# The tap load moved from SyncE's queue to the head of GpSimd's queue

## The chip, the cores and the metric

The kernel runs on one core of a Trainium2 chip. The metric is the device time of one execution in microseconds (us). The core has five engines with a queue of instructions each: TensorE (PE in the profile; its weight loads are PEld), VectorE (DVE), ScalarE (ACT), GpSimd (POOL) and SyncE (SP). Engines wait for each other, and for transfers, through semaphores. Transfers (DMAs) are issued by SyncE, ScalarE or GpSimd and carried out by 16 DMA engines that all of them share.

## The reference

The inputs are `x` of shape (8, 4096, 192), `weight` of shape (8, 7), `w_in` (192, 2048) and `w_out` (2048, 192), all float32. The output has shape (32768, 192).

```
w   = softmax(weight, axis=-1)                    # 8 heads x 7 taps
att[b, s, h*24 + g] = sum_k w[h, k] * x_padded[b, s + k, h*24 + g]    # causal, 6 zeros ahead
h   = att.reshape(32768, 192) @ w_in              # 2048 wide
g   = where(h > 0, h, exp(min(h, 0)) - 1)         # ELU
out = g @ w_out
```

So it is a short convolution along the sequence with seven softmax weights per head, then two matrix products with an ELU between them.

## The kernel before, in words

The 32768 tokens are cut into 32 blocks of 1024. For each block the kernel makes the convolved tokens (`att`), multiplies them with 16 column groups of `w_in` (the matmuls at L749, into PSUM tiles `H`), applies the ELU in three steps (ScalarE takes the exponential into `E` at L543, GpSimd clips it to at most 1 at L471, VectorE combines it with `H` into `gT` at L610), and multiplies `gT` with `w_out` (L783). The order of TensorE's matmuls is written out once, in the list `steps`, and the other engines follow the same list, so that the second product and the convolution of later blocks are fitted between the matmuls of the first product.

The convolution itself is done on TensorE in two ways. The very first block takes a short way, called the head here: its x is loaded in two halves of 512 tokens into `xf` (the function `load_first`, L340; ScalarE's queue takes half 0, SyncE's half 1), cast to bfloat16 into `xh` (ScalarE at L490 half 0, VectorE at L578 half 1), transposed by TensorE (L649 for the few halo columns, L662 for the rest), copied to `xT`, and multiplied with `Dg`, which holds the taps on diagonals (L682). All later blocks use a banded matrix `Tm`, made from the taps through a small DRAM buffer `conv_taps`, and x tiles `xg` (L727).

The taps are needed by both ways. They start as `wh`, an 8 x 7 float32 tile loaded from `weight`. The softmax is run by VectorE and ScalarE in turn: maximum (L562), difference (L564), exponential (ScalarE, L488), reciprocal (L568), product into `zt` (L570). When `zt` is there, TensorE spreads it to all partitions (L643, after nine warm-up matmuls at L638), VectorE builds `Dg`, and SyncE writes it to `conv_taps` (L805), waits for that, and loads `Tm` (L810).

Each engine does its own work in order, which sets the following sequences around the change:

- SyncE: load of `wh`, load of half 1 of the first x, store of zeros to `conv_taps` (waits for VectorE's `zw`), store of the taps (waits for `zt`), load of `Tm`, and then the loop over `steps` with loads of x, transposes of `att` and stores of the output.
- GpSimd: two selects that make the identity matrix `ident` (L431) and the spreading matrix `sel` (L440), a wait until `wh` has landed (`W(s_wd, 16)`), six loads of `w_in` (L425), two of `xg` for block 1 (L398), the load of `w_out`, two of `xg` for block 2, and then the loop of clips, with copies of x to bfloat16 in DRAM in between.
- VectorE: six memsets, `mask` (waits for `ident`), a wait for `s_wd`, the softmax steps, the cast of half 1 of x, `Dg`, and copies.
- ScalarE: load of half 0 of x, a table load, the exponential of the softmax (waits for VectorE), the cast of half 0, and copies.

The semaphore `s_wd` counts the landing of `wh`; GpSimd and VectorE wait for it. The semaphores `s_xl[0]` and `s_xl[1]` count the landings of the two halves of the first x, `s_wp` the end of `zt`.

Of the kernel before, what the change touches and what calls it, by code (L numbers as in the profile page):

```python
# [54 lines left out]
def bass_lightweight_conv__then__act_elu_kernel(  # L55
# [167 lines left out]
    with ExitStack() as stack:  # L223
        def sbuf(name, shape, dt):
            return stack.enter_context(nc.sbuf_tensor(name, shape, dt))
# [4 lines left out]
        def sema(name):  # L230
            return stack.enter_context(nc.semaphore(name))
# [6 lines left out]
        wh = sbuf("wh", [HEADS, KSIZE], FP32)  # L238
# [23 lines left out]
        s_wd = sema("s_wd")  # L262
# [50 lines left out]

        def x_ready(W, s, part):
            if s <= NXB:
                W(s_x[s % NXB][part], 16)
            else:
                W(s_xq[s % NXB][part], 32 * ((s - 1) // NXB))

# [24 lines left out]

        def conv_read(W, m):
            W(s_ce, 2 * (m + 1))

# [16 lines left out]

        def singles_done(W, acc):
            x_ = final[acc]
# [26 lines left out]
        @block.gpsimd  # L393
        def _gpsimd(g: bass.BassGpSimd):
            W = Waits(g)

            def load_x(s, part):
                g.dma_start(  # L398
                    xg[:, s % NXB, WPG * part : WPG * (part + 1), :],
                    bass.AP(  # L400
                        tensor=x_flat.tensor,
                        offset=(s * SUP + GS * part - PAD) * D,
                        ap=[[D, P], [TOK * D, WPG], [1, D]],
                    ),
                ).then_inc(s_x[s % NXB][part], 16)

            def pad_x(s):
                x_ready(W, s, 0)
                g.memset(xg[0:PAD, s % NXB, 0, :], 0.0).then_inc(s_z)

            def copy_x(s):
                W(s_cv, 4 * (s - NXB - 1) + 1)
                if s == NXB + 1:
                    g.dma_start(  # L414
                        xb[s * SUP - 8 : s * SUP, :], x_flat[s * SUP - 8 : s * SUP, :]
                    ).then_inc(s_xb[s % 2], 16)
                g.dma_start(  # L417
                    xb[s * SUP : (s + 1) * SUP, :].rearrange("(p t) d -> p (t d)", p=P),
                    x_flat[s * SUP : (s + 1) * SUP, :].rearrange("(p t) d -> p (t d)", p=P),
                ).then_inc(s_xb[s % 2], 16)  # L420

            def load_w_in(k, halves):
                c0, c1 = WCOLS[k]
                for r in halves:
                    g.dma_start(  # L425
                        w_in[HP * r : HP * (r + 1), :, c0:c1],
                        moe_w_in.rearrange("(p j) f -> p j f", j=3)[:, :, c0:c1],
                    ).then_inc(s_w[k], 16)

            W(s_one, 1)  # L430
            g.affine_select(  # L431
                out=ident[:],
                in_=ident[:],
                pattern=[[-1, P]],
                compare_op=ALU.is_equal,
                fill=0.0,
                base=0,
                channel_multiplier=1,
            ).then_inc(s_id)
            g.affine_select(  # L440
                out=sel[:].rearrange("p (r h c) -> p r h c", r=2, h=HEADS),
                in_=sel[:].rearrange("p (r h c) -> p r h c", r=2, h=HEADS),
                pattern=[[0, 2], [-1, HEADS], [0, 8]],
                compare_op=ALU.is_equal,
                fill=0.0,
                base=0,
                channel_multiplier=1,
            ).then_inc(s_id)
            W(s_wd, 16)
            load_w_in(0, (0, 1))  # L450
            load_w_in(1, (0, 1))
            load_w_in(2, (0, 1))
            load_x(1, 0)
            load_x(1, 1)
            g.dma_start(
                w_out.rearrange("p (q r) d -> p q (r d)", r=RUN),
                moe_w_out.rearrange("(q p r) d -> p q (r d)", p=FC, r=RUN),
            ).then_inc(s_w[3], 16)
            load_x(2, 0)
            load_x(2, 1)  # L460
            for n in range(NP):
                s, i = divmod(n, NQ)
                if i == X_PAD and s + 2 < NS and (s + 2) % SPB == 0:
                    pad_x(s + 2)
                if i == X_COPY and s and s + 3 < NS:
                    copy_x(s + 3)
                if n == X_LATE[0]:
                    copy_x(3)
                for u in range(2):
                    W(s_exp, 2 * n + u + 1)  # L470
                    g.tensor_scalar(  # L471
                        out=E[:, n % NE, u, :],
                        in0=E[:, n % NE, u, :],
                        scalar1=1.0,
                        scalar2=0.0,
                        op0=ALU.min,
                        op1=ALU.max,
                    ).then_inc(s_clp)
# [315 lines left out]
        @block.sync  # L794
        def _sync(sy):
            W = Waits(sy)
            sy.dma_start(wh[:], weight[:, :]).then_inc(s_wd, 16)
            load_first(sy, 1)
            W(s_zw, 1)
            sy.dma_start(  # L800
                bass.AP(tensor=taps.tensor, offset=0, ap=[[(HEADS + 2) * CW, BANDS], [(HEADS + 1) * CW, 2], [1, CW]]),
                zw[0:BANDS, 0 : 2 * CW].rearrange("p (a e) -> p a e", a=2),
            ).then_inc(s_band, 16)
            W(s_wp, 1)
            sy.dma_start(  # L805
                bass.AP(tensor=taps.tensor, offset=CW, ap=[[CW, HEADS], [(HEADS + 2) * CW, BANDS], [1, CW]]),
                zt[:, :].unsqueeze(1).to_broadcast([HEADS, BANDS, CW]),
            ).then_inc(s_band, 16)
            W(s_band, 32)
            sy.dma_start(  # L810
                Tm[:, :, :].rearrange("p h e -> p (h e)"),
                bass.AP(tensor=taps.tensor, offset=CW + TAP + KSIZE - 1, ap=[[(HEADS + 2) * CW - P // BANDS, BANDS], [-1, P // BANDS], [1, HEADS * CW]]),
            ).then_inc(s_band, 16)

            def load_cast(s):
                W(s_cv, 4 * (s - NXB))
                W(s_xb[s % 2], 16 * ((s - 1) // 2 + (s % 2)))
                if s > NXB + 1:
                    W(s_xb[(s - 1) % 2], 16 * ((s - 2) // 2 + ((s - 1) % 2)))
                for part in range(2):  # L820
                    row = s * SUP + GS * part - PAD
                    for w0, w1, rows in ((0, WPG - 1, P), (WPG - 1, WPG, GS - TOK * (WPG - 1) + PAD)):
                        v0 = WPG * part
                        sy.dma_start(
                            xg[0:rows, s % NXB, v0 + w0 : v0 + w1, :],
                            bass.AP(
                                tensor=xb.tensor,
                                offset=(row + TOK * w0) * D,
                                ap=[[D, rows], [TOK * D, w1 - w0], [1, D]],
                            ),  # L830
                        ).then_inc(s_xq[s % NXB][part], 16)

            for x_, op in enumerate(steps):
                if op[0] == "h" and op[2:] == (0, 0):
                    s, i = divmod(op[1], NQ)
                    if i == X_LOAD and s and s + 3 < NS:
                        load_cast(s + 3)
                    if op[1] == X_LATE[1]:
                        load_cast(3)
                elif op[0] == "c" and op[3:] == (1, HB - 1):  # L840
                    m, b = op[1:3]
                    s = m // 2 + 1
                    if m % 2 and b:
                        conv_read(W, m)
                        for u in range(2):
                            W(s_h[u], NQ * (s - 1))
                        turn_att(sy, s)
                elif x_ in stops:
                    acc = acc_of(op)
                    t, half, kb, g = acc  # L850
                    if (t, half) == (last, 1):
                        if (kb, g) != (1, 1):
                            taken(W, acc)
                            out_group(sy, t, half, g, kb)
                    else:
                        taken(W, acc)
                        out_group(sy, t, half, g)
            for b in range(2):
                sy.wait_ge(s_out[b], 32 * NS + 32 * b)
# [28 lines left out]
```

## Time and profile before

| | |
|---|---|
| time, median of 3 runs | 726.29 us (725.12 to 727.17) |
| the profiled execution's own time | 724.59 us |
| its span in the profile | 722.5 us |
| TensorE busy | 714.7 us, 99% of the span |
| ScalarE, VectorE, GpSimd busy | 91%, 90%, 87% |
| granted TensorE clock | 1.0 |
| issue of `wh` (SyncE's queue), start and length | 0.80 us, 0.40 us |
| issue of half 1 of the first x (SyncE's queue) | 1.26 us, 0.36 us |
| issue of half 0 of the first x (ScalarE's queue) | 0.81 us, 0.38 us |
| GpSimd's first load of `w_in` | 2.44 us |

The span is the time between the first and the last recorded instruction; the time of a run is a little longer than that. Starts are counted from the beginning of the span. "SPq" and "ACTq" in a row are the queues of SyncE and ScalarE, where only the issue of a transfer is shown and not the transfer; a row of GpSimd for a DMA likewise shows the issue. A bracket at the end of a row gives how long the engine had been idle and what ended that. In the lists of DMA queues, q0 carries what GpSimd issues.

### The profile page before, as it was taken

The numbers are of one execution on the slowest core, as the hardware profiler recorded it, in microseconds if no ns is written. First come the engines' busy times: TensorE is split into PE (matmuls) and PEld (weight loads), VectorE is DVE, ScalarE is ACT, GpSimd is POOL, SyncE is SP. The second block draws the span as 40 slices with busy tenths as digits, with TensorE's granted clock in tenths as the row PEclk, the third lists the DMA queues.
The fourth block names the chain that finished last, engine by engine and source line by source line (L and its number), as shares of the span: only waits on it lengthen the run. The fifth ranks groups of instructions, "written<-read, shape, count | busy, mean of one in ns | idle before, by whom it ended". The sixth has DMA issues, their size and how long they took to land.

```text
span 722.5 us, 28723 instructions
## 1 busy us (share of the span) xinstructions
PE 714.7 (99%) x11866; PEld 620.3 (86%) x11866; DVE 651.1 (90%) x1043; ACT 655.9 (91%) x1286; POOL 631.0 (87%) x1078
## 2 busy tenths in 40 slices
PE   8899999999999999999999999999999999999997
PEld 4598888888888888888888888888888888888897
DVE  5899999999999999999999999999999999999994
ACT  6899999999999999999999999999999999999994
POOL 8889988889888889888889888898888898888893
PEclk9999999999999999999999999999999999999999
DMA  9854533654534644444645335545346455432212
GB/s 179 129 117 86 112 78 88 117 103 83 103 83 95 116 91 96 94 93 95 116 82 106 83 83 116 105 82 111 75 95 117 93 93 100 88 94 71 58 36 67
DMA packets 130051, 69.16 MB, mean 96 GB/s; under 512 B 94128, under 2 KB 128688, under 8 KB 129456
## 3 DMA queue, kind: packets, MB, share of 16 engines
q1 hardware_dynamic: 123760, 52.08, 30.5%
q0 software_dynamic: 5872, 14.75, 14.9%
q8 instruction: 93, 1.52, 0.9%
q10 hardware_dynamic: 288, 0.49, 0.2%
q14 instruction: 38, 0.31, 0.1%
HBM read 43.51 MB, written 36.61 MB: 111 GB/s over the span
## 4 chain that ended last, share of the span: by engine, by line
PE 95%; DMA 2%; POOL 1%; ACT 1%; issue 0%; DVE 0%; ACTq 0%
PE ops L783 51%; PE H L749 40%; PE H L727 3%; DMA xg<-in_x_dram 2%; PE H L783 1%; POOL w_in L425 1%; POOL E L471 1%; ACT E L543 0%; DVE gT L610 0%; POOL xg L398 0%; ACT csb L521 0%; POOL x_cast L414 0%; POOL x_cast L417 0%; POOL sel L440 0%; ACT osb L513 0%
## 5 line engine op out<-in xcount | busy, mean ns | idle before, releaser
L610 DVE SCALAR_TENSOR_TENSOR gT<-E,H 128x512 f16<-128x512 f32 x1024 | 645.3, 683 | 56.9 <-POOL E L471 49.7
L471 POOL TENSOR_SCALAR E<-E 128x512 f32<-128x512 f32 x1024 | 606.1, 616 | 79.5 <-ACT E L543 75.6
L543 ACT ACTIVATE E<-H 128x512 f32<-128x512 f32 x1024 | 565.2, 612 | 49.5 <-PE H L749 44.9
L749 PE MATMUL H<-att,w_in 64*128 64x512 bf16 x3072 | 602.9, 377 | 1.2 <-DVE gT L610 1.0
L783 PE MATMUL ops<-w_out,gT 64*128 64x192 f16 x8064 | 587.0, 243 | 0.0
L783 PEld LDWEIGHTS ops<-w_out,gT 64*128 64x128 f16 x8064 | 516.5, 94 | 54.5 <-PE ops L783 29.4
L749 PEld LDWEIGHTS H<-att,w_in 64*128 64x128 bf16 x3072 | 258.0, 94 | 20.0 <-DVE gT L610 6.5
L727 PE MATMUL H<-xg,Tm 64*128 64x240 bf16 x480 | 87.6, 263 | 0.3 <-DVE gT L610 0.3
L521 ACT ACTIVATE csb<-H 128x480 bf16<-128x480 f32 x120 | 70.7, 589 | 0.0
L513 ACT ACTIVATE osb<-ops 128x384 f32<-128x384 f32 x125 | 61.0, 488 | 7.3 <-PE ops L783 5.7
L727 PEld LDWEIGHTS H<-xg,Tm 64*128 64x128 bf16 x480 | 38.2, 93 | 16.1 <-issue 0.6
L417 POOL DMA_DIRECT2D x_cast<-in_x_dram x29 | 15.6, 538 | 0.0
L783 PE MATMUL H<-w_out,gT 64*128 64x192 f16 x128 | 6.4, 243 | 0.0
L783 PEld LDWEIGHTS H<-w_out,gT 64*128 64x128 f16 x128 | 5.7, 94 | 0.0
L638 PE MATMUL ops<-zw 128*128 128x512 bf16 x9 | 4.0, 631 | 1.2 <-DVE zw L553 1.2
L602 DVE COPY osb<-ops 128x384 f32<-128x384 f32 x1 | 0.6, 558 | 4.3 <-PE ops L783 4.3
L727 PE MATMUL ops<-xg,Tm 64*128 64x240 bf16 x16 | 3.0, 264 | 1.3 <-ACT csb L521 0.7
L699 PE MATMUL ops<-zw 64*128 64x512 bf16 x12 | 4.2, 376 | 0.0
L425 POOL DMA_DIRECT2D w_in<-in_moe_w_in_dram x6 | 4.0, 664 | 0.2 <-DMA wh<-in_weight_dram 0.2
L638 PEld LDWEIGHTS ops<-zw 128*128 128x128 bf16 x9 | 1.2, 143 | 3.2 <-issue 1.9
L727 PEld LDWEIGHTS ops<-xg,Tm 64*128 64x128 bf16 x16 | 0.9, 94 | 3.2 <-ACT csb L521 1.5
L398 POOL DMA_DIRECT2D xg<-in_x_dram x4 | 3.5, 878 | 0.0
(49 smaller groups left out, 29.8 us busy)
## 6 DMA issues: line engine op xcount, KB each, us to landing
out_dram<-osb SPq DMA_DIRECT2D x126, 192.0 KB, 3.3
x_cast<-in_x_dram POOLq DMA_DIRECT2D x29, 384.0 KB, 5.1
xg<-x_cast SPq DMA_DIRECT2D x58, 192.0 KB
xg<-x_cast SPq DMA_DIRECT2D x58, 26.2 KB
xg<-in_x_dram POOLq DMA_DIRECT2D x4, 240.0 KB, 13.3
w_in<-in_moe_w_in_dram POOLq DMA_DIRECT2D x2, 384.0 KB, 10.4
w_out<-in_moe_w_out_dram POOLq DMA_DIRECT2D x1, 768.0 KB, 14.6
w_in<-in_moe_w_in_dram POOLq DMA_DIRECT2D x2, 288.0 KB, 6.3
```

Source lines behind the costliest of these rows:

```text
L417: g.dma_start(xb[s * SUP : (s + 1) * SUP, :].rearrange("(p t) d -> p (t d)", p=P), x_flat[s * SUP : (s + 1) * SUP, :].rearrange("(p t) d - ...
L425: g.dma_start(w_in[HP * r : HP * (r + 1), :, c0:c1], moe_w_in.rearrange("(p j) f -> p j f", j=3)[:, :, c0:c1],).then_inc(s_w[k], 16)
L471: g.tensor_scalar(out=E[:, n % NE, u, :], in0=E[:, n % NE, u, :], scalar1=1.0, scalar2=0.0, op0=ALU.min, op1=ALU.max,).then_inc(s_clp)
L513: a.activation(*out_pieces(acc), ACT.Copy).then_inc(s_oev)
L521: return a.activation(csb[:, s % 2, :].rearrange("p (j v h i) -> p h j v i", j=3, v=2 * WPG, h=HEADS)[:, h0 : h0 + HB], bank_of(("c", m, b ...
L543: a.activation(E[:, n % NE, u, :], bank_of(op[:3]), ACT.Exp).then_inc(s_exp)
L610: v.scalar_tensor_tensor(out=gT[:, s % NG3, q, u, :], in0=E[:, n % NE, u, :], scalar=1.0, in1=bank_of(op[:3]), op0=ALU.subtract, op1=ALU.m ...
L638: pe.matmul(ops[:, 0, :], zw[:, 0:P], zw[:], start=True, stop=True)
L699: pe.matmul(ops[:, 1 - rt, :], zw[HP * rt : HP * (rt + 1), 0:P], zw[HP * rt : HP * (rt + 1), :], start=True, stop=True, tile_position=(HP ...
L727: ins = pe.matmul(bank_of(op[:3])[:, n1 * hh : n1 * (hh + 1)], Tm[HP * rt : HP * (rt + 1), h, :], xg[HP * rt : HP * (rt + 1), s % NXB, :, ...
L749: ins = pe.matmul(bank_of(op[:3]), w_in[HP * r : HP * (r + 1), j, RUN * FC * (q // RUN) + q % RUN : RUN * FC * (q // RUN + 1) : RUN,], att ...
L783: ins = pe.matmul(to[:, d0 : d0 + D], gT[HP * rt : HP * (rt + 1), t % NG3, q, g, t0 : t0 + P], w_out[HP * rt : HP * (rt + 1), q, :], start ...
```

## The change

The load of `wh` is taken out of SyncE's queue, where it was the first instruction, and put into GpSimd's queue as its first instruction of the kernel body. Its source, its destination and the semaphore it raises stay the same. SyncE now begins with half 1 of the first x load; GpSimd issues one more transfer, ahead of its two selects, and later still waits for that transfer where it did before. Every line number between the two places grows by one.

```diff
@@ -393,6 +393,7 @@
         @block.gpsimd
         def _gpsimd(g: bass.BassGpSimd):
             W = Waits(g)
+            g.dma_start(wh[:], weight[:, :]).then_inc(s_wd, 16)
 
             def load_x(s, part):
                 g.dma_start(
@@ -794,7 +795,6 @@
         @block.sync
         def _sync(sy):
             W = Waits(sy)
-            sy.dma_start(wh[:], weight[:, :]).then_inc(s_wd, 16)
             load_first(sy, 1)
             W(s_zw, 1)
             sy.dma_start(
```

## The prediction

> **What bounds the kernel now.** I read the page first: TensorE is busy 99% of the span, and 95% of the chain that ended last is matmuls. So most of this kernel can't notice a change at its start, except as a shift of everything. Whether the start is on the path at all is told by the chain of waits in order of time, cut to the first 40 us (start, length, what):
>
> ```profile
> 1.83 0.36 POOL sel L440
> 2.20 0.24 issue
> 2.44 0.84 POOL w_in L425
> ...
> 3.27 3.11 POOL w_in L425 x5
> 6.39 0.90 POOL xg L398
> 7.29 11.57 DMA xg<-in_x_dram
> 18.86 0.14 issue
> 19.00 0.26 PE ops L727
> ```
>
> The head of the path is not the first x load. It is GpSimd: its two selects, six `w_in` loads, the two `xg` loads, then the landing of `xg` at 18.86, for which TensorE stands idle 0.53 us in front of the first convolution matmul (L727). From there the chain goes through the exponentials to 31 us and then stays on TensorE to the end. `load_w_in` stands behind GpSimd's wait for the taps (`s_wd`), so the taps' landing is directly ahead of this path.
>
> The timeline of the first 6 us shows both sides of the edit (start, length, engine, line):
>
> ```profile
> 0.80 0.40 SPq L797 DMA_DIRECT2D wh<-in_weight_dram  x1
> ...
> 1.26 0.36 SPq L340 DMA_DIRECT2D xf<-in_x_dram  x1
> ...
> 2.16 0.15 DVE L562 TENSOR_REDUCE whm<-wh 8x1 f32<-8x7 f32 x1
> ...
> 2.86 0.19 ACT L488 ACTIVATE whe<-wh 8x7 f32<-8x7 f32 x1
> ...
> 3.36 0.22 DVE L570 TENSOR_SCALAR zt<-whe,whr 8x7 bf16<-8x7 f32 x1
> ...
> 3.92 0.84 ACT L490 ACTIVATE xh<-xf 128x768 bf16<-128x768 f32 x1 [0.78 <-DMA xf<-in_x_dram]
> ...
> 5.08 0.56 DVE L578 CAST xh<-xf 128x768 bf16<-128x768 f32 x1 [1.50 <-DMA xf<-in_x_dram]
> ...
> 5.21 0.18 PE L643 MATMUL H<-zt,sel 8*128 8x7 bf16 x1
> ```
>
> The taps, sent at 0.80, have landed by 2.16, when VectorE's reduction runs: at most 1.36 us. SyncE's half of x is cast at 5.08, yet TensorE only leaves its nine warm-up matmuls at 5.2 and still has the tap broadcast (L643) and twelve small halo matmuls ahead of the transposes that read that half.
>
> Last, the table by stretches (stretch, length, busy time of PE, PEld, DVE, ACT, POOL, granted clock, DMA share, GB/s), and then, from the list of DMA queues between 4.0 and 4.4 us, the packets of GpSimd's queue, their MB and their share:
>
> ```profile
> 1.50:2.00 0.50, 0.50 (x2) 0.15 (x1) 0.27 (x3) 0.50 (x1) 0.46 (x2) 1.00 0.52 80
> 2.00:2.50 0.50, 0.50 (x2) 0.15 (x1) 0.47 (x3) 0.50 (x1) 0.26 (x2) 1.00 0.65 166
> ...
> 3.50:4.00 0.50, 0.50 (x3) 0.16 (x2) 0.08 (x1) 0.07 (x1) 0.50 (x2) 1.00 1.03 418
> ...
> 17.00:18.00 1.00, 0.79 (x7) 0.21 (x5) 1.00 (x3) 0.80 (x2) 1.00 (x3) 1.00 1.52 196
> ```
>
> ```profile
> q0 software_dynamic: 22, 0.01, 27.7%
> ```
>
> The DMA engines are idle before 1.5 us, half used to 2.5 and full from then to 24. So `xg` lands when the work queued before it is done; only idle time of the DMA engines in the first microseconds can move it.
>
> **What the Trainium skill says.** "DMA: Bandwidth & Descriptors", section Specifications, puts the first byte at about 1 us on GpSimd's path and 0.6 on SyncE's. Its section "Anatomy of one DMA — SWDGE (gpsimd) path" gives a GpSimd DMA a fixed 2.0 us, mostly the receipt. The trace agrees in kind: a 3 KB copy of GpSimd (`x_cast`, L414) landed 2.8 us after its issue, while the taps by SyncE took 1.36 or less. "Issuing engines are not separate DMA queues" on the same page says that all queues end on the same 16 engines, as the full table shows. "SBUF — State Buffer", section "SBUF: two separate sides", warns that a VectorE operation in a two-port mode keeps GpSimd from writing descriptors. Here VectorE's 0.56 us cast at 5.08 ran beside GpSimd's `w_in` issues and none of those is over 0.84, so I price that at 0 to 0.5 us, inside the bounds below.
>
> **The change part by part.**
>
> *Removed from SyncE: one issue.* Its x load moves from 1.26 to about 0.80, 0.46 us. The engines had (0.48 + 0.35) x 0.5 = 0.41 us free between 1.5 and 2.5; I let x fill all of it. SyncE's x then lands near 4.6. ScalarE's half loses its head start and may land up to 0.5 later, at 4.4.
>
> *Added to GpSimd: one issue of 0.59 (L414) to 0.84 us (the first `w_in` issue, 0.21 longer than the median 0.63).* It starts near 0.8, so the select of `ident`, at 1.54 now, moves to at most 1.7. GpSimd also has an instruction without a row, which the build names a library reload; it stands just before that select, now after the new DMA. In the kernel before it fits between 0.8 and 1.54, so it costs 0 to 0.7. Even then `ident` and `sel` are done by 3.1; VectorE's mask waits for `ident` and TensorE (5.2) for both. They are hidden under the wait for the taps.
>
> *The taps land later.* Latency: lower end 1.36 + 0.4 (the skill's difference in first byte) = 1.8; upper end 3.2, that of the first 96 KB `w_in` load. I take 2.8, from L414: though that one writes to DRAM, the taps now travel while x has the engines full. Landing 3.6 (2.6 to 4.0).
>
> *Behind the taps on VectorE and ScalarE.* From the reduction at 2.16 to the end of `zt` at 3.58 takes 1.42, so `zt` is ready at 5.0 where TensorE wants it at 5.2: hidden by the warm-up, 0.4 late at the upper end. ScalarE's exponential moves to 4.3, and its cast of x behind it from 3.92 to 4.6, ending 5.45; the halo matmuls start 0.15 late. VectorE's cast goes from 5.08 to 5.0. The head thus gains nothing from the earlier x load, and may lose 0.15 (0.6 at the upper end). The first layer-one matmul at 9.9 may shift by that; it is covered by the 0.53 us that TensorE waits for `xg` anyway. SyncE's tap stores and `Tm` load, behind the same `zt`, move 1.4 later; `Tm`'s packets now end before 15, four microseconds before use.
>
> *Behind the taps on GpSimd: six w_in loads, two xg loads, w_out, two xg loads, then its clips.* The first issue moves from 2.44 to 3.6 + 0.24 = 3.84, or +1.4. It is no longer the first on its queue, which gives back 0.21. So GpSimd's packets start 1.2 later, at about 5.25 instead of 4.05. The x traffic left at 4.05 was some 0.26 us of work (65.7% of the 0.4 us stretch, on SyncE's queue); with 0.41 done earlier it ends at 3.9. The engines then idle 5.25 - 3.9 = 1.35, less the 0.41 saved: `xg` lands 0.9 later. Ends: -0.1 at a latency of 1.8, +1.3 at 3.2. `w_in`'s second part, wanted after 12 us, lands about 11 now, a cover of 1 us; `xg` for the next block lands about 25, wanted 26.9, and both move together.
>
> *To the end.* TensorE waits for `xg` with every later matmul behind it, and from 19 to 31 us the chain has no stall long enough to take up 0.9. All of it passes: span 722.5 + 0.9 = 723.4; the profiled execution took 724.59, 2.1 around its span, so 725.5. The median shown, 726.29, stands 1.7 above that execution, so the forecast is 727.2.
>
> **Rivals.** (a) *Hidden after all*: the taps by GpSimd land near 2.6, GpSimd's start hardly moves, and the DMA queue decides. For it: the transfer is 224 bytes. Against it: L414. Time 726.3. (b) *The edit does what its words say*: x half a microsecond earlier and `xg` earlier with it. TensorE could use at most the 0.53 it waits for `xg`: 725.8. Against it: GpSimd's loads would have to start no later than now. (c) *Slower*: the library reload can't begin while GpSimd's own DMA is open. It then starts at 3.6, takes up to 0.7, the selects 0.65, the issue 0.24: `w_in` at 5.2, 2.75 later. GpSimd's packets start at 6.6, idle 6.6 - 3.9 - 0.41 = 2.3, time 728.6. It decides for slower when the first `w_in` issue comes after 5.1; no row shows the reload, so I can't exclude it.
>
> **How the numbers follow.** A measurement of this kernel tells about 0.3%, 2.2 us. Chances: main case 0.6, (a) 0.15, (b) 0.05, (c) 0.15, and 0.05 for something later in the taps' landing than I bound. Only (c), the last and a little of the main case's upper end pass +2.2: slower 0.19; faster 0.03; same 0.78. The range reaches from (b), less run-to-run scatter (725.1 to 727.2 before), to (c): 725.3 to 729.0.
>
> **What would show it.** Right: the reduction on VectorE at about 3.6, GpSimd's first `w_in` at 3.8, TensorE leaving the warm-up at 5.2 still, `xg` landing near 19.8, a longer TensorE wait there, and nothing else changed from 31 us on but the shift. Wrong: the reduction before 2.8, or `ident`'s select after 3, or `xg` landing unchanged while `w_in` starts late, or a shift at 20 us that is gone at 31.

## The result and the profile after

The changed kernel takes 730.08 us in the median of four runs (729.92 to 730.36), the kernel before 726.48 us in four (725.12 to 727.17): a ratio of 1.0052, 95% interval 1.0035 to 1.0070. It is slower by 3.6 us, where 0.9 had been forecast. Of the two profiled executions the one after has a span of 728.1 us, the one before 722.5; that one (724.59 us by its own time) was at the quick end of its kernel, so the difference of the spans, 5.6 us, is larger than that of the medians.

Nearly the whole loss, 5.3 of these 5.6 us, is made in the first 37 us. The chain of waits of the changed kernel, its first 40 us (start, length, what):

```profile
1.34 4.15 DMA wh<-in_weight_dram
...
5.79 3.97 POOL w_in L426 x6
9.76 0.89 POOL xg L399
10.65 13.54 DMA xg<-in_x_dram
...
24.33 0.26 PE ops L728
```

The path goes the same way as before, through GpSimd's loads to the landing of `xg`, but with the taps now at its head: 4.15 us from their issue to their landing at 5.49, where they had landed by 2.16. `w_in` starts 3.35 us later (5.79 for 2.44) and `xg` lands 5.33 later (24.19 for 18.86). The point of the chain where VectorE hands over to TensorE for good is at 36.4 us instead of 31.1. From 40 to 700 us TensorE is busy without a gap in both kernels.

The timeline of the first 7 us, the main rows that answer to those shown of the kernel before:

```profile
0.80 0.39 SPq L340 DMA_DIRECT2D xf<-in_x_dram  x1
...
1.34 0.68 POOL L396 DMA_DIRECT2D wh<-in_weight_dram  x1 [0.83 <-POOLq L873]
...
5.51 0.15 DVE L563 TENSOR_REDUCE whm<-wh 8x1 f32<-8x7 f32 x1 [2.77 <-DMA wh<-in_weight_dram]
...
6.83 0.16 PE L644 MATMUL H<-zt,sel 8*128 8x7 bf16 x1 [1.85 <-DVE zt L571]
```

GpSimd starts its issue at 1.34, half a microsecond after the other two queues; no row shows why. VectorE then waits 2.77 us for the taps, and everything behind it is late: both casts of x (ScalarE's at 6.16 for 3.92, VectorE's at 6.61 for 5.08), and TensorE's tap broadcast at 6.83 instead of 5.21, in front of which TensorE is idle for 1.85 us.

The DMA engines, by the list of DMA issues of the first 3.4 us (KB, us from issue to landing):

```profile
xf<-in_x_dram SPq DMA_DIRECT2D x1, 384.0 KB, 4.2
xf<-in_x_dram ACTq DMA_DIRECT2D x1, 384.0 KB, 4.3
wh<-in_weight_dram POOLq DMA_DIRECT2D x1, 0.2 KB, 4.2
```

and by the same list of the kernel before:

```profile
xf<-in_x_dram ACTq DMA_DIRECT2D x1, 384.0 KB, 3.1
xf<-in_x_dram SPq DMA_DIRECT2D x1, 384.0 KB, 3.8
```

Both halves of x now land at about 5.0 to 5.1 us. Before, they landed at 3.9 and 5.1. So SyncE's half, sent 0.46 us earlier, is there no more than 0.1 us earlier, and ScalarE's half is 1.2 us later. The taps, 224 bytes, land after both.

The table by stretches (columns as in the prediction) shows what that does to the engines that carry the rest. First a row of the kernel before, then rows of the changed one:

```profile
5.00:5.50 0.50, 0.50 (x5) 0.28 (x5) 0.42 (x1) 0.00 (x0) 0.50 (x2) 1.00 0.99 120
```

```profile
5.00:5.50 0.50, 0.00 (x0) 0.00 (x0) 0.00 (x0) 0.00 (x0) 0.00 (x0) 1.00 0.00 0
...
6.00:7.00 1.00, 0.16 (x1) 0.09 (x1) 0.69 (x3) 0.98 (x3) 1.00 (x2) 1.00 0.00 0
...
8.00:9.00 1.00, 0.99 (x19) 0.74 (x15) 0.62 (x1) 0.79 (x2) 1.00 (x2) 0.50 1.05 140
```

The DMA engines, full from 2.5 to 24 us in the kernel before, are empty from 5 to 7 us: x is done, and `w_in`, whose issue only starts at 5.79, shows its first packets at 7.2. TensorE's granted clock (the third figure from the right) falls to half from 8 us, after its idle stretch.

### The profile page after: what moved, and what is told of

The parts are those of the page before. It is cut to its first block, busy times and chain, and to the rows that moved or that the text cites. A ratio compares the mean times of both kernels' runs of the same rounds, so it can differ in the third digit from the quotient of the medians.

```text
span 728.1 us, 28723 instructions
## 1 busy us (share of the span) xinstructions
PE 716.0 (98%) x11866; PEld 621.2 (85%) x11866; DVE 651.6 (89%) x1043; ACT 655.9 (90%) x1286; POOL 631.8 (87%) x1079
## 4 chain that ended last, share of the span: by engine, by line
PE 95%; DMA 2%; POOL 1%; ACT 1%; issue 0%; DVE 0%; ACTq 0%; POOLq 0%
PE ops L784 51%; PE H L750 40%; PE H L728 3%; DMA xg<-in_x_dram 2%; PE H L784 1%; DMA wh<-in_weight_dram 1%; POOL w_in L426 1%; ACT E L544 1%; POOL E L472 0%; POOL xg L399 0%; ACT csb L522 0%; DVE gT L611 0%; POOL x_cast L418 0%; POOL x_cast L415 0%; ACT osb L514 0%
## 5 line engine op out<-in xcount | busy, mean ns | idle before, releaser
L784 PEld LDWEIGHTS ops<-w_out,gT 64*128 64x128 f16 x8064 | 516.5, 94 | 54.5 <-PE ops L784 29.4
L750 PEld LDWEIGHTS H<-att,w_in 64*128 64x128 bf16 x3072 | 258.4, 94 | 21.3 <-DVE gT L611 3.6
```

The source lines that it names most:

```text
L750: ins = pe.matmul(bank_of(op[:3]), w_in[HP * r : HP * (r + 1), j, RUN * FC * (q // RUN) + q % RUN : RUN * FC * (q // RUN + 1) : RUN,], att ...
L784: ins = pe.matmul(to[:, d0 : d0 + D], gT[HP * rt : HP * (rt + 1), t % NG3, q, g, t0 : t0 + P], w_out[HP * rt : HP * (rt + 1), q, :], start ...
```

## The experiments

Two theories of the late taps. A: they share the DMA engines with x, and land with x when they are not ahead of it. B: a first transfer by GpSimd's queue is slow by itself. And two theories of how the delay reaches the end. G: through GpSimd's wait in front of its loads. H: through the late softmax at the head.

### The taps alone on the DMA engines

```diff
 # changed kernel; SyncE, and ScalarE after its table load:
+W(s_wd, 16)
 load_first(...)
```

> The changed kernel, but both halves of the first x are sent only once the taps have landed. If the taps land late because they share the DMA engines with x (theory A), they now land about 2.0 to 2.6 us after GpSimd's issue at 1.34, at 3.4 to 3.9. If a first transfer by GpSimd is slow by itself (theory B), they land where they do in the changed kernel, at about 5.5. The total is no test here, since x comes some 3 us late: 729 to 732 under A.

728.63 us in its one run, beside 725.88 for the kernel before. The chain of waits of this kernel:

```profile
1.33 1.76 DMA wh<-in_weight_dram
3.11 4.43 DMA xf<-in_x_dram
```

By the same queue, from the same start, the taps land at 3.09: 1.76 us after the issue instead of 4.15. So GpSimd's path isn't what is slow; of the 4.15 us, 2.4 go with x being ahead. Its landing is even quicker than theory A had asked. The edit holds back SyncE's store of zeros as well, to 3.55; that this small store isn't the cause is shown by the next run, where it is sent behind the taps and they are late all the same. The second line tells the price of this cure: x itself, landing at 7.54, is now the head of the path. Still, with x 2.4 us later than in the changed kernel, the one run of this kernel is no slower than it.

### The exchange on SyncE's queue, without GpSimd

```diff
 # kernel before, SyncE
-sy.dma_start(wh[:], weight[:, :]).then_inc(s_wd, 16)
 load_first(sy, 1)
+sy.dma_start(wh[:], weight[:, :]).then_inc(s_wd, 16)
```

> The kernel before with two instructions of SyncE's queue exchanged: its half of x first, then the taps; GpSimd issues nothing more. If taps sent beside or behind x land late whatever the queue (theory A), they land near 5, w_in starts near 5.3 and the time is about 729.5 to 730. If GpSimd's path is what is slow (theory B), they land 1.3 us after an issue at 1.25, near 2.6, and the time is 726.5 to 727.

730.58 us (730.34 to 731.12), 1.0063 of the kernel before, interval 1.0048 to 1.0078. The chain of waits, and then VectorE's reduction in the timeline:

```profile
1.24 4.08 DMA wh<-in_weight_dram
```

```profile
5.35 0.15 DVE L562 TENSOR_REDUCE whm<-wh 8x1 f32<-8x7 f32 x1 [3.19 <-DMA wh<-in_weight_dram]
```

The taps take 4.08 us on SyncE's queue too when x goes first, and the whole loss is there, 4.7 us against the kernel before (725.88), with GpSimd's queue untouched. With the first experiment this settles A against B from both sides.

### The taps first on ScalarE's queue

```diff
 # kernel before: taken from SyncE's queue; ScalarE begins with
+a.dma_start(wh[:], weight[:, :]).then_inc(s_wd, 16)
 load_first(a, 0)
```

> The kernel before with the taps at the head of ScalarE's queue instead of SyncE's: SyncE begins with its half of x at 0.80, the taps are first in the other queue, ScalarE's half follows at 1.26. If what counts is that the taps are in a queue ahead of x's packets (theory A), they land near 2.1 and the time is that of the kernel before within 0.7 us. If x sent at the same moment by another queue is enough to hold them back, they land near 5 and the time is about 730.

726.09 us (725.43 to 727.64), 1.0004 of the kernel before, interval 0.9996 to 1.0013: no difference. The chain of waits:

```profile
1.41 3.92 DMA xf<-in_x_dram
...
5.36 0.85 ACT xh L491
...
6.26 0.64 PE H L650 x9
```

VectorE's reduction runs at 2.16, as before, though SyncE's x is sent at 0.80, at the same moment as the taps. So x may be sent beside the taps, not ahead of them. It also bears on what the change wanted: SyncE's half of x goes first here with the taps on time, and nothing is won. But ScalarE's half, from which the halo matmuls are made, goes 0.6 us later for it (1.41 for 0.81), lands at 5.34 and is the head of the path. What SyncE's half would be worth with ScalarE's left where it was isn't tested.

### GpSimd's wait alone

```diff
 # kernel before, GpSimd, with a tile wg and a semaphore s_wg of its own
+g.dma_start(wg[:], weight[:, :]).then_inc(s_wg, 16)
 ...
-W(s_wd, 16)
+W(s_wg, 16)
 load_w_in(0, (0, 1))
```

> The kernel before, with a second copy of the taps loaded at the head of GpSimd's queue into a tile of its own; GpSimd waits for that copy before its w_in loads, and the softmax uses SyncE's copy as before. If GpSimd's late loads carry the loss (theory G), xg lands 3 to 5 us later and the time is about 730, as in the changed kernel, though the softmax is on time. If the late head carries it (theory H alone), the time stays at 726.5.

729.16 us (728.77 to 729.59), 1.0044, interval 1.0028 to 1.0061. Theory G carries 3.3 us with the softmax as good as on time (the tap broadcast is at 5.20). But it isn't `xg` that ends the chain here:

```profile
1.33 3.87 DMA wg<-in_weight_dram
...
7.44 8.70 DMA w_in<-in_moe_w_in_dram
...
16.19 0.39 PE H L752
...
20.65 0.65 PE H L752 x3
```

TensorE, at its first layer-one matmul at 10.49 (10.02 in the kernel before), then waits 3.8 us for the second part of `w_in`. The matmuls after this wait are on the chain too, and from 18 to 20 us their granted clock is 0.50. So a part of the 3.3 us may be the clock's; no run separates the two. The copy of the taps by GpSimd lands at 5.2 here with both x loads where they were in the kernel before: again with x, which was sent ahead of it.

### The head alone: no wait on GpSimd

```diff
 # changed kernel, GpSimd
-W(s_wd, 16)
 load_w_in(0, (0, 1))
```

> The changed kernel without GpSimd's wait for the taps before its loads of w_in; VectorE still waits for them. If the loss goes through GpSimd's loads alone (theory G), w_in starts near 3.0, xg lands near 19.5 and the time is that of the kernel before, 726.5 to 727. If the late softmax at the head carries part of it too (theory H), TensorE reaches its first layer-one matmul near 12.7 instead of 10.0, the convolution about 2.1 us later than before, and the time is about 728.5.

727.81 us (727.41 to 728.46), 1.0025, interval 1.0016 to 1.0035. With GpSimd's loads nearly on time 1.9 us are left, between what G and H had said. The chain shows a third way that neither had:

```profile
1.34 4.37 DMA wh<-in_weight_dram
...
6.93 8.27 DMA conv_taps<-zt
15.22 6.53 DMA Tm<-conv_taps
```

`zt` is late, so SyncE's store of the taps is sent at 6.9, now behind GpSimd's `w_in` packets, takes 8.27 us for 32 KB, and the `Tm` load behind it lands at 21.75, when `xg` has been there for three microseconds. TensorE's wait for it is short, though:

```profile
21.79 0.27 PE L727 MATMUL ops<-xg,Tm 64*128 64x240 bf16 x1 [0.50 <-DMA Tm<-conv_taps]
```

TensorE comes to this place at 21.3 us, where it came at 18.5 in the kernel before. So the late softmax costs about 2 us by itself. `Tm` ends the chain, but by this trace it adds only 0.5 us to the late head, theory H. The head is late by the softmax, and from 9 to 11 us it runs at a clock of 0.50.

### The first cut of TensorE's clock

```diff
-WARM = (9, 1)
+WARM = (13, 1)      # changed kernel
```

> The changed kernel with 13 warm-up matmuls on TensorE in place of 9, so that TensorE is busy until the late taps come, at about 6.7, and its clock is not cut to half from 8 to 11.4 us. If the head is off the path (xg ends it), TensorE reaches its first layer-one matmul about 1 us earlier, near 11.6, and the time stays that of the changed kernel, within 0.5 us of 730. If the cut clock is part of the loss, the time falls by 1 us or more, to 729 or less.

729.92 us (729.80 to 730.17), 1.0056, interval 1.0041 to 1.0071, against 730.08 of the changed kernel. The row of the table by stretches:

```profile
8.00:9.00 1.00, 0.67 (x20) 0.55 (x17) 0.69 (x1) 0.92 (x3) 1.00 (x2) 1.00 1.18 148
```

The clock is whole there now, the first layer-one matmul is at 11.47 instead of 12.66, and the time doesn't move: this cut of the clock and the late head are off the path in the changed kernel. A second cut comes after the wait for `w_in` and stands in both kernels (0.50 from 19 to 21 us). In the changed kernel it is over before TensorE waits 0.83 us for `xg`, so the chain doesn't go through it; the second run of the next experiment doesn't have it.

### xg ahead of the last part of w_in

```diff
 # GpSimd
 load_w_in(1, (0, 1))
-load_w_in(2, (0, 1))
 load_x(1, 0)
 load_x(1, 1)
+load_w_in(2, (0, 1))
```

On the kernel before:

> The kernel before with GpSimd's two xg loads for block 1 ahead of the last part of w_in. In the kernel before TensorE waits 0.53 us for xg; here xg should land near 14 and the last part of w_in near 18.9, wanted near 19.3. A gain of 0.3 to 0.6 us if nothing else binds; none, if the last part of w_in takes xg's place.

724.85 us (723.70 to 726.62), 0.9983, interval 0.9977 to 0.9990: 0.9 us won, a little more than expected, and below both kernels. `xg` is off the path, and in its place stands the very thing the change was after, SyncE's half of x:

```profile
1.25 4.22 DMA xf<-in_x_dram
...
5.49 0.94 DVE xh L578
...
6.48 0.45 PE H L662 x8
```

On the changed kernel:

> The changed kernel with GpSimd's two xg loads for block 1 ahead of the last part of w_in, the same exchange that was worth 0.9 us on the kernel before. If xg alone carries the late start of GpSimd's loads to the end, most of the loss is gone and the time is near 727. If the second part of w_in, for which TensorE waits 2.2 us at 17.1 in the changed kernel, carries it as well, only the 0.8 us that TensorE waits for xg after that is won, and the time is near 729.2: 4.4 above the kernel before with the same exchange.

729.66 us (728.90 to 730.81), 1.0049, interval 1.0036 to 1.0061. That is 0.4 us under the changed kernel's 730.08, and the loss against the kernel before (726.09 here) is still 3.6. In the changed kernel TensorE waits for the second part of `w_in` and then for `xg`:

```profile
17.14 0.39 PE L750 MATMUL H<-att,w_in 64*128 64x512 bf16 x1 [2.22 <-DMA w_in<-in_moe_w_in_dram]
...
24.33 0.26 PE L728 MATMUL ops<-xg,Tm 64*128 64x240 bf16 x1 [0.83 <-DMA xg<-in_x_dram]
```

With `xg` ahead, the chain of waits goes through the second part of `w_in`:

```profile
7.99 9.55 DMA w_in<-in_moe_w_in_dram
17.59 0.39 PE H L750
...
19.77 4.88 DVE gT L611 x8
```

The granted clock is 1.00 from 17 to 24 us, so the loss is there without the second cut of the clock. This part of `w_in` lands at 17.54 us here. By the increments of its semaphore it landed at 17.09 in the changed kernel and at 11.77 in the kernel before. So the late start of GpSimd's loads reaches the end by two ways, and taking one away leaves the other.

### The wait itself, on the kernel before

```diff
 # kernel before, GpSimd
-W(s_wd, 16)
 load_w_in(0, (0, 1))
```

> The kernel before without GpSimd's wait for the taps. The taps land at 2.14 there, before GpSimd has done its two selects at 2.20, so the wait should cost nothing: w_in starts near 2.4 and the time is that of the kernel before within 0.7 us.

725.79 us (724.97 to 726.46), 1.0000, interval 0.9991 to 1.0009. While the taps are first, the wait costs nothing; it only makes GpSimd's loads hostage to their landing.

## Why the prediction was wrong

The forecast was 727.2 with a range to 729.0; measured are 730.1.

**The taps land later: the step that failed.** "Landing 3.6 (2.6 to 4.0)" came from a latency of 2.8, bounded above by 3.2. Measured: 4.15, from an issue at 1.34 and not at 0.80, landing 5.49. Of the 1.9 us between 3.6 and 5.49 the latency makes 1.35 and the later issue 0.54. The step saw that the taps "travel while x has the engines full" and then took its numbers from rows in which that holds less. The 2.8 was a copy at 28.6 us, during which the DMA engines were nearly idle from 29.4 to 30.3. The 3.2 was the first `w_in` load, issued at 2.44, only 2.6 us ahead of x's landing; it landed at 5.6, itself just behind x. In every kernel here in which the taps were sent behind x, the end of x is what bounded them. In the profile before that number could be read: x landed at 5.06. Issue at 1.34, landing with x at about 5.1 to 5.5, would have given `w_in` at 5.3 to 5.8, and by the prediction's own rival (c), which "decides for slower when the first `w_in` issue comes after 5.1", a slower kernel.

**Removed from SyncE: an assumed gain.** "I let x fill all of it", 0.41 us of free DMA time. Nothing came of it: SyncE's half landed at most 0.1 us earlier, and ScalarE's half 1.2 later against the allowed 0.5. The last packet of x begins at 4.58 us, in the kernel before at 4.50; the sum had x done at 3.9.

**Behind the taps on VectorE and ScalarE.** The 1.42 us from reduction to `zt` was near in size (5.51 to 6.68 after, 1.17), but its cover, the warm-up to 5.2, was gone: TensorE stood idle 1.85 us, and from 8 us its clock was cut. That this head is covered by the wait for `xg` held in the changed kernel (the experiment with more warm-up). It doesn't hold once `xg` is on time: without GpSimd's wait the late softmax costs 1.9 us. There `Tm`, "four microseconds before use" in the prediction, had no cover left, with the tap store queued behind `w_in`.

**Behind the taps on GpSimd.** The path was right: `w_in`, then `xg`, then everything. With the right landing the sum of the prediction gives: packets of GpSimd from about 7.2, x done at 3.9, idle 3.3, less 0.41: 2.9, and a time of 729.2; between the medians 3.6 were measured. The 0.41 is the gain that didn't come. `xg` itself was 5.33 later in the profiled executions, more than the idle time of the DMA engines explains (last section). The cover of 1 us claimed for the second part of `w_in` was used up too, and TensorE waited 2.2 us for it.

**To the end.** "All of it passes" was right: 5.33 us at `xg` became 5.34 where TensorE takes over the chain, and 5.6 of span.

**The rivals.** (a) and (b) are refuted: GpSimd's loads started 3.35 us later and the time rose. (c) named the right place with the wrong cause: `ident`'s select runs at 2.12, right after GpSimd's issue and three microseconds before the taps land, so no instruction of GpSimd was held by its open DMA. The time fell to the case given 0.05, "something later in the taps' landing than I bound".

## What to carry to other kernels

A small transfer that many engines wait for belonged ahead of the large ones in time here, on SyncE's queue or on ScalarE's: sent 0.5 us after 768 KB of x had been issued, 224 bytes landed with the end of x, by GpSimd's queue and by SyncE's alike. When a transfer's latency has to be bounded, take the row that was issued into the same traffic, and if there is none, take the end of that traffic. A wait that costs nothing today (GpSimd's, 0.0 us) still ties the loads behind it to what it waits for, so price it by what happens when that comes late.

## What the runs showed that was not expected

The taps landed after x even on a queue of their own. In the list of DMA queues GpSimd's packets, issued by 2.02, first appear between 4.0 and 4.5 us, as x runs out (q1 and q10 carry SyncE's and ScalarE's transfers):

```profile
q10 hardware_dynamic: 41, 0.11, 55.0%
q1 hardware_dynamic: 46, 0.06, 34.3%
q0 software_dynamic: 10, 0.00, 1.1%
```

The Trainium skill ("DMA: Bandwidth & Descriptors", section "Queues, rings and completion order") says that each engine takes the queues in turn by packet, and that the write that raises the semaphore lands only after every earlier write of that engine, across its queues. The second fits every kernel in which the taps were sent behind x: by the semaphores in the trace they landed at 5.3 to 5.7 us (their copy at 5.2), each 0.2 to 0.4 after x. It doesn't explain the delay, which is already in the packets. Whether the first explains it these traces can't tell, for they show neither single DMA engines nor how many rows a turn takes. GpSimd's next load fares alike: the first `w_in`, issued at 2.44 in the kernel before, shows its first packet at 4.1, and with the taps alone, issued at 3.38 behind x, at 6.7. Why they come so late was not tested.

The landing of `xg`'s second half is counted by sixteen increments of a semaphore. They spread over 1.7 us in the kernel before (17.18 to 18.86) and over 3.4 in the changed one (20.82 to 24.19). The first is 3.6 us later, nearly as much as the loads are, and the last 5.3. So part of the difference between the two profiled executions is a longer tail of this landing. It is no accident of one execution: the other two kernels in which taps and loads are both late, with the same order of loads, show 3.9 (the exchange on SyncE's queue) and 3.0 us (more warm-up). With GpSimd's wait alone it is 2.2, and in the kernels whose loads start on time, with the same order, 1.7 to 2.4. What makes the tail longer is open.
